# Where the operands of a float32r MLP start in SBUF, with a fourth buffer for v, stores planned on their own and an earlier guard

## The chip, the cores and the metric

The kernel runs on one core of a Trainium2 chip. The metric is the device time of one execution in microseconds. Before the change the median of three runs is 556.32 us (555.0 to 556.47). The profile shown here is of one more execution, which took 556.87 us, 554.8 us of it between its first and its last instruction (the span); the other 2.1 us lie around the span.

## The reference

The reference is a linear attention with decay (B=4 sequences, H=8 heads, S=768 tokens, D=48 per head), whose output goes through an MLP of model width 384 and hidden width 2048.

```python
for t in range(S):
    cur = einsum('bhd,bhe->bhde', u * k[t], v[t])
    y[t] = einsum('bhd,bhde->bhe', r[t], state + cur)
    state = w[t] * state + einsum('bhd,bhe->bhde', k[t], v[t])
x = y as [3072 tokens, 384]
h = x @ w_in
g = where(h > 0, h, exp(min(h, 0)) - 1)
out = g @ w_out
```

All inputs and the output are float32 (the weights arrive as 64-bit floats and are converted in the kernel).

## The kernel before

**Tiling.** Time is cut into 6 blocks of 128 steps (the code's `c`). A block has 4 units, one a sequence, so there are 24 units; a unit does the attention of 128 steps for all heads, and the four units of a block give the 512 token columns on which the MLP of that block works.

**Attention of a unit.** The loads w, k, r, v (and rk from unit 8 on) go out on SP's queue. VectorE runs two scans over the decays (lines 344 and 354) and scales r and k (358 and 361). TensorE makes the scores pa_s (413); VectorE masks them into am (416); TensorE makes the output pa_y from am, v and the carried state (443), the transposes pa_t (421), and the outer products pa_u (460) that VectorE adds to the state (468). pa_y is split into xh, rounded to float32r (ScalarE, 449), and the remainder xl (VectorE, 453).

**MLP of a block.** Each of the 16 slices f of the hidden width is a step with two groups of nine matmuls. `g1` (227 to 229) makes ph from xh and xl: for each of three 128-row chunks, w_h with xh, w_h with xl, w_l with xh. The ELU runs on ScalarE and VectorE (233, 236, 239), and the result m is split into gh (243) and gl (247). `g2` (256 to 258) adds nine matmuls of the same pattern to three accumulators acc. The moving operand is 512 columns wide (2048 bytes of a partition); in blocks 0 and 1 the first 6 slices are done as two halves of 256 columns. The weights of slice f are converted while block 0 runs (487 to 509). When a block is done, acc is copied to o and stored (269, 270); in the kernel before, each store is issued by the same task as its copy, so it stands in SP's queue right where the copy stands in the order of work.

**The order of work** is written by a list scheduler in the kernel (`Plan.order`). Each operation is a task with an engine, a duration (`COST`), predecessors, buffers that it takes (`hold`, with the counts in `SLOTS`) and a due time worked back from `BEGINS`, the planned begins of the six blocks. The scheduler simulates the engines with these numbers, and the instructions are issued in the order that results, on SP's queue too. At run time nothing is reordered: an engine or queue waits at its next instruction.

**Where tiles lie.** Pools are laid out in SBUF in the order of their creation. In the program built from the kernel before, the first tile of a pool lies at byte 16,512 of each partition. From the sizes of the tiles follow these begins, as remainders of 2048 bytes; a w_h or w_l operand is one of the 512-byte pieces of its tile:

| operand | before | after |
|---|---|---|
| w_h, w_l (pieces of 512 bytes) | 128, 640, 1152, 1664 | 0, 512, 1024, 1536 |
| xh, xl of blocks 0, 2, 4 | 896, 896 | 0, 0 |
| xh, xl of blocks 1, 3, 5 | 1056, 1152 | 0, 0 |
| gh, gl (two buffers each) | 1088 | 0 |

**The guard.** A product of the decays that is too small would make the scans wrong; `flag` collects a sum per unit, and `guard` (511 to 516) adds the sums up and writes `good`. After the fast part every engine loads `good` (line 655) and branches past a slow general version of the kernel.

Of the kernel before, what the change touches and what calls it, by code (L numbers as in the profile page):

```python
# [64 lines left out]
BEGINS = (20.6, 125.1, 205.2, 299.0, 400.1, 445.7, 557.5)
SOON = 0.0
LEAD = 70.0
ND = 8  # L70
SLOTS = dict(w=2, k=3, r=3, rk=2, v=3, eg=2, md=2, am=2, kt=1, pa=3, wg=2, ph=2, m=2, gh=2, gl=2, x=2, acc=1, raw0=1, x0=1, x1=1, x1a=1, x1b=1)


class Plan:
# [15 lines left out]
    def order(self):  # L90
# [29 lines left out]
        server = 0.0  # L120
# [5 lines left out]
        while len(order) < len(ts):  # L126
            moved = False
            for e in ready:
# [3 lines left out]
                for k in ready[e]:  # L132
# [6 lines left out]
                    u = (t["late"], rank[k])  # L139
# [22 lines left out]
                end = now + t["dur"]  # L162
# [49 lines left out]
def mlp(nc, w_h, w_l, ps_acc, ps_h, ml, po, dst, last=False):  # L212
# [9 lines left out]
    def g1(s, x):  # L222
        f, lo, hi = s["f"], s["lo"], s["hi"]
        xh, xl = (z[:, :, lo:hi] for z in x)
        s["ph"] = ph = ps_h.tile([P, N], F32, tag="ph", name="ph")[:, 0:hi - lo]
        for k in range(NK):
            nc.tensor.matmul(ph, w_h[:, f, 0, k], xh[:, k, :], start=(k == 0), stop=False)  # L227
            nc.tensor.matmul(ph, w_h[:, f, 0, k], xl[:, k, :], start=False, stop=False)  # L228
            nc.tensor.matmul(ph, w_l[:, f, 0, k], xh[:, k, :], start=False, stop=(k == NK - 1))  # L229
# [11 lines left out]
    def gh(s):  # L241
        s["gh"] = ml.tile([P, N], F32R, tag="gh", name="gh", bufs=2)[:, 0:s["hi"] - s["lo"]]
        nc.scalar.copy(s["gh"], s["m"])  # L243

    def gl(s):
        s["gl"] = ml.tile([P, N], F32R, tag="gl", name="gl", bufs=2)[:, 0:s["hi"] - s["lo"]]
        nc.vector.tensor_tensor(s["gl"], s["m"], s["gh"].bitcast(F32), ALU.subtract)  # L247

    def g2(s):
        f, lo, hi = s["f"], s["lo"], s["hi"]  # L250
        for m in range(NK):
            parts = 2 if (f == NF - 1 and m == NK - 1 and last) else 1
            for q in range(parts):
                s_ = slice(q * (hi - lo) // parts, (q + 1) * (hi - lo) // parts)
                a_ = accs()[m][:, lo + s_.start:lo + s_.stop]
                nc.tensor.matmul(a_, w_h[:, f, 1, m], s["gh"][:, s_], start=(f == 0 and lo == 0), stop=False)  # L256
                nc.tensor.matmul(a_, w_h[:, f, 1, m], s["gl"][:, s_], start=False, stop=False)  # L257
                nc.tensor.matmul(a_, w_l[:, f, 1, m], s["gh"][:, s_], start=False, stop=(f == NF - 1 and q == parts - 1))  # L258
# [3 lines left out]
    def out(m):  # L262
# [4 lines left out]
        for q in range(parts):  # L267
            s_ = slice(q * N // parts, (q + 1) * N // parts)
            (nc.vector.tensor_copy if last and (m == 1 or q) else nc.scalar.copy)(o[:, m, s_], acc[m][:, s_])
            nc.sync.dma_start(dst[m * P:(m + 1) * P, s_], o[:, m, s_])  # L270

    return dict(g1=g1, r1=r1, r2=r2, stt=stt, gh=gh, gl=gl, g2=g2, out=out)


@with_exitstack
def rwkv_elu_kernel(ctx, tc, wkr, rk, vp, u, uz, gkrw, gv, gu, w_in, w_out, out):
# [207 lines left out]
    def conv_a(f):  # L484
        g = stg.tile([P, 2, NK, P], U32, tag="wg", name="wg", bufs=2)
# [22 lines left out]
    def conv_l(f, eng):  # L508
        eng.tensor_tensor(w_l[:, f], raws[f][1].bitcast(F32), w_h[:, f].bitcast(F32), ALU.subtract)  # L509
# [19 lines left out]
    for u_ in units:  # L529
        i, c, b = u_["i"], u_["c"], u_["b"]  # L530
        early = max(0.0, BEGINS[c] - LEAD) if c > 0 else 0.0
        for n, kb in (("w", 232), ("k", 229), ("r", 229), ("rk", 393), ("v", 262)):
            if n == "rk" and i < ND:
# [9 lines left out]
        if i < ND:  # L543
# [4 lines left out]
            add(("md", i), "ACT", K["md"], lambda u_=u_: diag_out(u_), [("pd", i)])  # L548
            add(("sp", i), "ACT", K["spa"], lambda u_=u_: spread_act(u_), [("md", i), ("const",)])
        else:  # L550
            e1, e2 = ENG(i)
            for n, e, fn, dep in (("rk", e1, r_k, [("ld_rk", i)]), ("rku", e2, r_k_u, [("rk", i), ("ub",)])):
                add((n, i), e, K[n if e == "DVE" else "p" + n],
                    lambda u_=u_, fn=fn, e=e: fn(u_, nc.vector if e == "DVE" else nc.gpsimd), dep, lock=True)
            add(("dg", i), "DVE", K["dg"], lambda u_=u_: diag(u_), [("rku", i)])
            add(("sp", i), "POOL", K["sp"], lambda u_=u_: spread(u_), [("dg", i)], lock=True)
# [209 lines left out]
```

## Time and profile before

| | us |
|---|---|
| median of 3 runs | 556.32 (555.0 to 556.47) |
| profiled execution | 556.87 |
| its span | 554.8 |
| TensorE busy in the span | 519.8 |
| VectorE busy | 362.5 |
| ScalarE busy | 285.6 |
| GpSimd busy | 69.9 |
| mean granted TensorE clock | 0.974 of full |

PE is TensorE's matmuls, PEld its weight loads, DVE VectorE, ACT ScalarE, POOL GpSimd, SP the engine whose queue issues the transfers (SPq). A matmul's row in the timeline has its start, its duration and its line; the durations of neighbours overlap, so the rate of TensorE is read from the distance between starts. In a row of the windows view, each engine has its busy time and its count of instructions, then come the granted TensorE clock (PEclk), the DMA engines' busy share and GB/s.

### The profile page before, as it was taken

How to read it: one execution, taken by the hardware profiler on the slowest of the kernel's cores; microseconds unless marked ns; L12 is line 12 of the kernel's file. 1: busy time of each engine (PE TensorE's matmuls, PEld its weight loads, DVE VectorE, ACT ScalarE, POOL GpSimd, SP SyncE). 2: the span in 40 equal slices, each digit the busy share in tenths (PEclk: the TensorE clock that was granted, in tenths of full speed). 3: DMA queues.
4: the chain of work that ended last, by engine and by line, in shares of the span. 5: the costliest groups of instructions: out<-in, count | busy, mean ns of one | idle time of the engine just before them, and what ended most of it. 6: DMA issues, size and time to landing. Idle time of an engine off the chain costs nothing.

```text
span 554.8 us, 10007 instructions
## 1 busy us (share of the span) xinstructions
PE 519.8 (94%) x4065; PEld 430.3 (78%) x4065; DVE 362.5 (65%) x565; ACT 285.6 (51%) x558; POOL 69.9 (13%) x72
## 2 busy tenths in 40 slices
PE   5875999999999999999999999998799999999993
PEld 5765898889998887787878788876578878888882
DVE  6899999998796375369377335987596345333331
ACT  3668587687665443455443445643274432534441
POOL 1000000000240011215002300704530001000000
PEclk9977999999999999999999999999699999999998
DMA  8863574034410036211036200226520011100001
GB/s 267 250 199 120 156 234 168 1 87 144 122 60 2 0 90 192 59 55 36 0 91 201 69 0 18 74 91 209 153 70 1 0 37 38 58 0 1 0 1 61
DMA packets 26739, 47.36 MB, mean 85 GB/s; under 512 B 2752, under 2 KB 9280, under 8 KB 26688
## 3 DMA queue, kind: packets, MB, share of 16 engines
q1 hardware_dynamic: 26688, 46.66, 27.3%
q8 instruction: 34, 0.56, 0.4%
q14 instruction: 17, 0.14, 0.1%
HBM read 41.93 MB, written 4.72 MB: 84 GB/s over the span
## 4 chain that ended last, share of the span: by engine, by line
PE 83%; DVE 7%; DMA 3%; issue 3%; ACT 2%; SPq 1%; DVEq 0%; ACTq 0%
PE acc L256 12%; PE ph L227 12%; PE ph L229 11%; PE ph L228 11%; PE acc L257 11%; PE acc L258 11%; PE pa_y L443 6%; PE pa_s L413 4%; PE pa_u L460 2%; DMA v<-in_vp_dram 1%; PE pa_d L385 1%; PE pa_t L421 1%; DMA ubd<-in_uz_dram 1%; DVE gl L247 1%; DVE am L416 1%
## 5 line engine op out<-in xcount | busy, mean ns | idle before, releaser
L239 DVE SCALAR_TENSOR_TENSOR m<-m,ph 128x512 f32<-128x512 f32 (+1 forms) x108 | 67.1, 624 | 106.2 <-ACT m L236 105.9
L227 PE MATMUL ph<-xh,w_h 128*128 128x512 f32 (+1 forms) x324 | 123.2, 380 | 3.6 <-ACT w_h L506 1.6
L233 ACT ACTIVATE m<-ph 128x512 f32<-128x512 f32 (+1 forms) x108 | 59.3, 549 | 124.0 <-PE ph L229 120.8
L229 PE MATMUL ph<-xh,w_l 128*128 128x512 f32 (+1 forms) x324 | 121.0, 373 | 1.9 <-DVE w_l L509 1.9
L256 PE MATMUL acc<-gh,w_h 128*128 128x512 f32 (+1 forms) x325 | 122.0, 375 | 0.0
L228 PE MATMUL ph<-xl,w_h 128*128 128x512 f32 (+1 forms) x324 | 121.1, 374 | 0.2
L257 PE MATMUL acc<-gl,w_h 128*128 128x512 f32 (+1 forms) x325 | 120.2, 370 | 0.0
L258 PE MATMUL acc<-gh,w_l 128*128 128x512 f32 (+1 forms) x325 | 120.0, 369 | 0.0
L247 DVE TENSOR_TENSOR gl<-m,gh 128x512 fp32r<-128x512 f32 (+1 forms) x108 | 70.8, 658 | 35.1 <-ACT gh L243 34.8
L243 ACT CAST gh<-m 128x512 fp32r<-128x512 f32 (+1 forms) x108 | 61.4, 570 | 49.9 <-DVE m L239 43.4
L227 PEld LDWEIGHTS ph<-xh,w_h 128*128 128x128 f32 x324 | 62.2, 192 | 17.8 <-DVE m L239 3.0
L229 PEld LDWEIGHTS ph<-xh,w_l 128*128 128x128 f32 x324 | 62.1, 192 | 13.4 <-DVE w_l L509 2.4
L256 PEld LDWEIGHTS acc<-gh,w_h 128*128 128x128 f32 x325 | 61.4, 189 | 12.7 <-issue 1.0
L228 PEld LDWEIGHTS ph<-xl,w_h 128*128 128x128 f32 x324 | 62.3, 192 | 11.4 <-DVE xl L453 0.8
L258 PEld LDWEIGHTS acc<-gh,w_l 128*128 128x128 f32 x325 | 61.4, 189 | 11.3
L257 PEld LDWEIGHTS acc<-gl,w_h 128*128 128x128 f32 x325 | 61.4, 189 | 11.3 <-DVE gl L247 0.3
L236 ACT ACTIVATE m<-m 128x512 f32<-128x512 f32 (+1 forms) x108 | 63.1, 584 | 3.1
L403 POOL TENSOR_SCALAR_AFFINE_SELECT am<-md 128x512 f32<-128x512 f32 x32 | 29.2, 934 | 221.7 <-PE pa_y L443 156.2
L416 DVE COPY_PREDICATED am<-upper,pa_s 128x512 f32<-128x512 uint32 x48 | 32.8, 737 | 13.0 <-PE pa_s L413 11.9
L368 POOL TENSOR_TENSOR rk<-rk 128x384 f32<-128x384 f32 x16 | 18.3, 1147 | 171.9 <-DMA rk<-in_rk_dram 171.9
L413 PE MATMUL pa_s<-r,k 48*128 48x128 f32 x384 | 31.9, 304 | 7.7 <-issue 6.4
L413 PEld LDWEIGHTS pa_s<-r,k 48*128 48x128 f32 x384 | 26.9, 204 | 13.4 <-issue 9.9
(61 smaller groups left out, 504.4 us busy)
## 6 DMA issues: line engine op xcount, KB each, us to landing
v<-in_vp_dram SPq DMA_DIRECT2D x24, 256.0 KB, 3.1
rk<-in_rk_dram SPq DMA_DIRECT2D x16, 384.0 KB, 3.7
w<-in_wkr_dram SPq DMA_DIRECT2D x24, 226.2 KB, 4.8
k<-in_wkr_dram SPq DMA_DIRECT2D x24, 224.0 KB, 3.1
r<-in_wkr_dram SPq DMA_DIRECT2D x24, 224.0 KB, 5.1
out_dram<-o SPq DMA_DIRECT2D x17, 256.0 KB, 2.1
wrawx<-in_w_in_dram SPq DMA_DIRECT2D x10, 384.0 KB, 3.9
wrawx<-in_w_out_dram SPq DMA_DIRECT2D x10, 384.0 KB, 4.5
```

What stands on the lines that cost most here:

```text
L227: nc.tensor.matmul(ph, w_h[:, f, 0, k], xh[:, k, :], start=(k == 0), stop=False)
L228: nc.tensor.matmul(ph, w_h[:, f, 0, k], xl[:, k, :], start=False, stop=False)
L229: nc.tensor.matmul(ph, w_l[:, f, 0, k], xh[:, k, :], start=False, stop=(k == NK - 1))
L233: act(s["m"], s["ph"], AF.Relu, scale=-1.0)
L236: act(s["m"], s["m"], AF.Exp, scale=-1.0)
L239: stt_(s["m"], s["m"], -1.0, s["ph"], ALU.add, ALU.max)
L243: nc.scalar.copy(s["gh"], s["m"])
L247: nc.vector.tensor_tensor(s["gl"], s["m"], s["gh"].bitcast(F32), ALU.subtract)
L256: nc.tensor.matmul(a_, w_h[:, f, 1, m], s["gh"][:, s_], start=(f == 0 and lo == 0), stop=False)
L257: nc.tensor.matmul(a_, w_h[:, f, 1, m], s["gl"][:, s_], start=False, stop=False)
L258: nc.tensor.matmul(a_, w_l[:, f, 1, m], s["gh"][:, s_], start=False, stop=(f == NF - 1 and q == parts - 1))
L413: nc.tensor.matmul(pa[q][:, p], u_["k"][rs, p, :], u_["r"][rs, p, :], start=True, stop=True)
```

## The change

Four things change together.

- **Begins.** The kept pool `kp` is created before `big`, takes in the small constants `lim`, `ident`, `upper` and `ubd`, and is filled up by a tile of 160 floats, so that w_h begins at a multiple of 2048. xh and xl get a pool of their own (`xp`) right behind the weights, gh and gl another (`gp`) behind that. The table above has the begins that result.
- **v.** `SLOTS` has four buffers for v in place of three, and a unit's `v` task comes after that of the unit before it in its block.
- **Stores.** For blocks 0 to 4 a store is a task of its own on SP, with a due time 20 us behind the begin of the next block; the buffer o is given back by the stores in the plan. In the last block the store of the first half of the third accumulator goes out on ScalarE's queue.
- **Guard.** Its due time is worked from the begin of the last block (`BEGINS[-2] + 15`) in place of the end (`BEGINS[-1] + 20`).

`BEGINS` has other numbers, and the first transfer of the plan starts at 1.0 us. Other new names have values that change nothing here: `COLS` is 128 (one pass of its loop), `FILL` is empty, `HALF`, `STAY` and `SWITCH` are 0, and `DIAG` and `SPREAD` say what `ND = 8` said. A wait for `wh` is added to what frees a `wg` buffer in the plan.

```diff
-BEGINS = (20.6, 125.1, 205.2, 299.0, 400.1, 445.7, 557.5)
+DMA_FIRST, DMA_ISSUE, DMA_LAT, DMA_RATE = 1.0, 0.45, 1.9, 215.0
+BEGINS = (16.7, 126.9, 219.0, 315.0, 381.0, 446.3, 528.1)
+COLS = 128
+PAD = 160
-SLOTS = dict(w=2, k=3, r=3, rk=2, v=3, ...)
+SLOTS = dict(w=2, k=3, r=3, rk=2, v=4, ...)
...
-            nc.tensor.matmul(ph, w_h[:, f, 0, k], xh[:, k, :], start=(k == 0), stop=False)
-            nc.tensor.matmul(ph, w_h[:, f, 0, k], xl[:, k, :], start=False, stop=False)
-            nc.tensor.matmul(ph, w_l[:, f, 0, k], xh[:, k, :], start=False, stop=(k == NK - 1))
+            for n, (w, x_) in enumerate(((w_h, xh), (w_h, xl), (w_l, xh))):
+                for z in range(0, P, COLS):
+                    nc.tensor.matmul(ph[z:z + COLS], w[:, f, 0, k, z:z + COLS], x_[:, k, :],
+                                     start=(k == n == 0), stop=(k == NK - 1 and n == 2))
...
-        s["gh"] = ml.tile([P, N], F32R, tag="gh", name="gh", bufs=2)[:, 0:s["hi"] - s["lo"]]
+        s["gh"] = gp.tile([P, N], F32R, tag="gh", name="gh", bufs=2)[:, 0:s["hi"] - s["lo"]]
...
-            nc.sync.dma_start(dst[m * P:(m + 1) * P, s_], o[:, m, s_])
+            if last:
+                (nc.scalar if m == NK - 1 and q == 0 else nc.sync).dma_start(dst[m * P:(m + 1) * P, s_], o[:, m, s_])
+    def store(m):
+        if not last:
+            nc.sync.dma_start(dst[m * P:(m + 1) * P], box["o"][:, m])
...
+    kp = keep("kp", 1)
     big = keep("big", 1)
-    kp = keep("kp", 1)
+    xp = pool("xp", 1)
+    gp = pool("gp", 2)
...
+    big.tile([P, PAD], F32, name="pad")
     w_h = big.tile([P, NF, 2, NK, P], F32R, name="w_h")
...
-    ident = cst.tile([P, P], F32, name="ident")
+    ident = kp.tile([P, P], F32, name="ident")
...
-            xts[c] = [at.tile([P, NK, N], F32R, tag=n + str(c % 2), name=n, bufs=1) for n in ("xh", "xl")]
+            xts[c] = [xp.tile([P, NK, N], F32R, tag=n + str(c % 2), name=n, bufs=1) for n in ("xh", "xl")]
...
+        if b:
+            after.append(("v", i - 1))
...
+            add(("store", c, m), "SP", DMA_ISSUE, lambda m=m, fns=fns: fns["store"](m), [("out", c, m)], due=BEGINS[c + 1] + 20, size=256)
...
-        hold("raw0", ("out", c, 0), [("out", c, m) for m in range(NK)])
-    add(("guard",), "PE", 0.3, guard, [("fl", i) for i in range(NU)], due=BEGINS[-1] + 20)
+        hold("raw0", ("out", c, 0), [("store", c, m) for m in range(NK)])
+    add(("guard",), "PE", 0.3, guard, [("fl", i) for i in range(NU)], due=BEGINS[-2] + 15)
```

More of the change, by code (lines that the diff above doesn't have):

```diff
@@ L138, in order @@
                         continue
-                    u = (t["late"], rank[k])
+                    u = (t["late"] + (STAY if e == "PE" and (k[0] in MODES) != (mode in MODES) else 0.0), rank[k])
                     if best is None or u < best[0]:
@@ L161, in order @@
                         users.setdefault(x, []).append(h)
-                end = now + t["dur"]
+                end = now + t["dur"] * (2.0 if e == "PE" and now < HALF else 1.0)
+                if e == "PE":
+                    end += SWITCH * (MODES.get(mode, 0) != MODES.get(k[0], 0))
+                    mode = k[0]
                 busy[e] = end
@@ L209, with mlp @@
 ROUNDS = value_rounds()
-def mlp(nc, w_h, w_l, ps_acc, ps_h, ml, po, dst, last=False):
+def mlp(nc, w_h, w_l, ps_acc, ps_h, ml, gp, po, dst, last=False):
     act, stt_ = nc.scalar.activation, nc.vector.scalar_tensor_tensor
@@ L255, in g2 @@
                 a_ = accs()[m][:, lo + s_.start:lo + s_.stop]
-                nc.tensor.matmul(a_, w_h[:, f, 1, m], s["gh"][:, s_], start=(f == 0 and lo == 0), stop=False)
-                nc.tensor.matmul(a_, w_h[:, f, 1, m], s["gl"][:, s_], start=False, stop=False)
-                nc.tensor.matmul(a_, w_l[:, f, 1, m], s["gh"][:, s_], start=False, stop=(f == NF - 1 and q == parts - 1))
+                for n, (w, g) in enumerate(((w_h, s["gh"]), (w_h, s["gl"]), (w_l, s["gh"]))):
+                    for z in range(0, P, COLS):
+                        nc.tensor.matmul(a_[z:z + COLS], w[:, f, 1, m, z:z + COLS], g[:, s_],
+                                         start=(f == n == 0 and lo == 0), stop=(f == NF - 1 and q == parts - 1 and n == 2))
     box = {}
@@ L409, in score @@
         u_["pa"] = pa = [ps_a.tile([P, NP, C], F32, tag="pa", name="pa_s") for q in range(2)]
+        for _ in range(FILL.get(("s", u_["i"]), 0)):
+            nc.tensor.matmul(pa[0][:, 0], ident, ident, start=True, stop=True)
         for p in range(NP):
@@ L506, in conv_h, with conv_l @@
         nc.scalar.copy(w_h[:, f], raws[f][1].bitcast(F32))
-    def conv_l(f, eng):
-        eng.tensor_tensor(w_l[:, f], raws[f][1].bitcast(F32), w_h[:, f].bitcast(F32), ALU.subtract)
+    def conv_l(f):
+        tt(w_l[:, f], raws[f][1].bitcast(F32), w_h[:, f].bitcast(F32), ALU.subtract)
     def guard():
@@ L532, in rwkv_elu_kernel @@
         for n, kb in (("w", 232), ("k", 229), ("r", 229), ("rk", 393), ("v", 262)):
-            if n == "rk" and i < ND:
+            if n == "rk" and DIAG[i] == "PE":
                 continue
@@ L548, in rwkv_elu_kernel @@
             add(("md", i), "ACT", K["md"], lambda u_=u_: diag_out(u_), [("pd", i)])
+        else:
+            e = DIAG[i]
+            for n, fn, dep in (("rk", r_k, [("ld_rk", i)]), ("rku", r_k_u, [("rk", i), ("ub",)])):
+                add((n, i), e, K[n if e == "DVE" else "p" + n],
+                    lambda u_=u_, fn=fn, e=e: fn(u_, nc.vector if e == "DVE" else nc.gpsimd), dep, lock=True)
+            add(("md", i), "DVE", K["dg"], lambda u_=u_: diag(u_), [("rku", i)])
+        if SPREAD[i] == "ACT":
             add(("sp", i), "ACT", K["spa"], lambda u_=u_: spread_act(u_), [("md", i), ("const",)])
         else:
[L551 to L556, printed above, removed]
+            add(("sp", i), "POOL", K["sp"], lambda u_=u_: spread(u_), [("md", i)], lock=True)
         add(("s", i), "PE", K["s"], lambda u_=u_: score(u_), [("rh", i), ("kh", i), ("sp", i)])
@@ L576, in rwkv_elu_kernel @@
         add(("a", f), "ACT", K["a"], lambda f=f: conv_a(f), [("raw", f, 0), ("raw", f, 1)])
[L577 to L580 removed]
+        add(("cand", f), "DVE", K["cand"], lambda f=f: conv_and(f), [("a", f)], lock=True)
         add(("cb", f), "DVE", K["cv"], lambda f=f: conv_b(f), [("cand", f)], lock=True)
@@ L588, in rwkv_elu_kernel @@
     for c in range(NC):
-        fns = mlp(nc, w_h, w_l, ps_acc, ps_h, ml, stg, out[:, c * N:(c + 1) * N], last=c == NC - 1)
+        fns = mlp(nc, w_h, w_l, ps_acc, ps_h, ml, gp, stg, out[:, c * N:(c + 1) * N], last=c == NC - 1)
         t = BEGINS[c]
@@ L595, in rwkv_elu_kernel @@
             dep = [("wl", f)] + [("xl", i) for i in ns] + [("xh", i) for i in ns]
-            add(("g1", n), "PE", K["g"] * part, lambda s=s, c=c, fns=fns: fns["g1"](s, xts[c]), dep + [("g1", n - 1)], due=t + K["g"] * part)
+            add(("g1", n), "PE", K["g"] * part, lambda s=s, c=c, n=n, fns=fns: fns["g1"](s, xts[c], [ident] * FILL.get(("g1", n), 0)), dep + [("g1", n - 1)], due=t + K["g"] * part)
             add(("r1", n), "ACT", K["r1"] * (part + 0.4) / 1.4, lambda s=s, fns=fns: fns["r1"](s), [("g1", n)])
@@ L632, in rwkv_elu_kernel @@
         hold(p, ("raw", f, 0), [("raw", f, 1), ("cb", f), ("cc", f)])
-        hold("wg", ("a", f), [("wl", f)])
+        hold("wg", ("a", f), [("wl", f), ("wh", f)])
         if p != "raw0":
@@ L706, in general @@
                 nc.vector.tensor_tensor(xl, xf, xh.bitcast(F32), ALU.subtract)
-                z = mlp(nc, w_h, w_l, ps_acc, ps_h, ml, ml, out[:, bass.ds(c * n, n)])
+                z = mlp(nc, w_h, w_l, ps_acc, ps_h, ml, ml, ml, out[:, bass.ds(c * n, n)])
                 for f in range(NF):
@@ L714, in general @@
                     z["out"](m)
+                    z["store"](m)
 _OUT = (DM, B * S)
```

55 lines of the change are left out of this document (25 added, 30 removed).

## The prediction

> **What bounds the kernel now.** I read the page's first part, then the engines' busy time cut at the first matmul of each block, then what TensorE waited for, then the distances between single matmuls.
>
> ```profile
> span 554.8 us, 10007 instructions
> PE 519.8 (94%) x4065; PEld 430.3 (78%) x4065; DVE 362.5 (65%) x565; ACT 285.6 (51%) x558; POOL 69.9 (13%) x72
> ```
>
> ```profile
> core 0: us, PE busy (x) PEld busy (x) DVE busy (x) ACT busy (x) POOL busy (x), PEclk, DMA share, GB/s
> ...
> 25.80:62.10 36.30, 25.96 (x244) 23.36 (x241) 34.31 (x54) 24.21 (x54) 0.00 (x0) 0.81 0.38 122
> 62.10:125.50 63.40, 62.66 (x483) 53.54 (x480) 61.37 (x97) 46.98 (x93) 0.00 (x0) 1.00 0.45 141
> 125.50:220.00 94.50, 93.53 (x939) 81.06 (x937) 66.34 (x111) 52.16 (x119) 14.96 (x16) 1.00 0.27 84
> 220.00:303.80 83.80, 82.92 (x657) 66.60 (x657) 53.51 (x81) 39.75 (x72) 18.20 (x16) 1.00 0.25 75
> 303.80:395.80 92.00, 86.33 (x673) 68.52 (x673) 56.12 (x84) 40.32 (x73) 23.81 (x22) 0.96 0.28 81
> 395.80:475.80 80.00, 80.00 (x609) 64.61 (x608) 48.62 (x75) 36.54 (x65) 10.62 (x10) 0.98 0.14 43
> 475.80:545.20 69.40, 69.40 (x303) 55.85 (x301) 22.08 (x32) 31.54 (x53) 0.00 (x0) 1.00 0.03 12
> ```
>
> These rows are block 0 in two parts and blocks 1 to 5. From block 1 on TensorE is the bound: it is busy nearly all the time, and VectorE is at 70% of a block at most (66.34 of 94.50), 32% in the last. Block 0 has a second bound: VectorE, which converts the weights there, is busy 34.31 of 36.30 us and 61.37 of 63.40. So a faster matmul pays in blocks 1 to 5 and hardly in block 0.
>
> ```profile
> PE pa_s L413 <- issue: 6.4, 1, 6.4
> PE pa_y L443 <- DMA v<-in_vp_dram: 4.3, 1, 4.3
> ```
>
> Of TensorE's waits the view names these two as the longest. The first is in block 0, the second, for a load of v, in block 3.
>
> **The rate of a matmul.** In the timeline of TensorE the first column is the start. These rows are the firsts of groups of nine matmuls, two rows 0.94 us apart with eight distances between them, and two rows in a stretch of half clock.
>
> ```profile
> 67.74 0.28 PE L227 MATMUL ph<-xh,w_h 128*128 128x256 f32 x1
> ...
> 68.68 0.28 PE L229 MATMUL ph<-xh,w_l 128*128 128x256 f32 x1
> ...
> 71.94 0.28 PE L256 MATMUL acc<-gh,w_h 128*128 128x256 f32 x1
> ...
> 72.96 0.28 PE L256 MATMUL acc<-gh,w_h 128*128 128x256 f32 x1
> ...
> 241.52 0.39 PE L227 MATMUL ph<-xh,w_h 128*128 128x512 f32 x1
> ...
> 243.56 0.39 PE L256 MATMUL acc<-gh,w_h 128*128 128x512 f32 x1
> ...
> 245.66 0.39 PE L227 MATMUL ph<-xh,w_h 128*128 128x512 f32 x1
> ...
> 247.72 0.39 PE L256 MATMUL acc<-gh,w_h 128*128 128x512 f32 x1
> ...
> 396.35 0.63 PE L228 MATMUL ph<-xl,w_h 128*128 128x512 f32 x1
> ...
> 398.91 0.60 PE L228 MATMUL ph<-xl,w_h 128*128 128x512 f32 x1
> ...
> 500.93 0.39 PE L227 MATMUL ph<-xh,w_h 128*128 128x512 f32 x1
> ...
> 503.02 0.39 PE L256 MATMUL acc<-gh,w_h 128*128 128x512 f32 x1
> ```
>
> Three things are to be seen. First, at half clock a 512-wide matmul comes every (398.91 - 396.35)/6 = 0.427 us; the same columns at full clock would take half, 213 ns. Second, at full clock none does: g1 of block 2 (xh and xl at 896) takes 2.04/9 = 227 ns in one step and 2.06/9 = 229 in the next, g1 of block 5 (1056 and 1152) 2.09/9 = 232, g2 (gh and gl at 1088) 2.10/9 = 233. The excess of 14 to 20 ns is absent at half clock, so it is not a fixed cost of an instruction in clock cycles; something that does not slow down with the clock feeds the array too slowly. Third, the excess goes with the begin of what streams: same instruction, shape and clock, and 227 against 233. The 256-wide ones come every 0.94/8 = 118 ns (x at 896) and 1.02/9 = 113 (g at 1088).
>
> **The begins.** What does a matmul cost with all operands at multiples of 2048? No row has it. Bounds: 213 below, the half of the slow rows; above, no gain (233), and for a collision worse than now, see the third rival. Between them: at begin 896 the second 256 columns of a 512-wide matmul cost 227 - 118 = 109 ns, the first 256 with everything fixed 118. If a good begin takes away the 9 ns by which the first half is dearer, a 512-wide one costs 218 and a 256-wide one 109. I take 218; it lies toward the lower bound, but the nearest row, 227, is already 6 ns under g2's with a begin that is no multiple of 2048, so a begin counts for that much at least.
>
> [...]
>
> The counts stand in the groups by line and shape:
>
> ```profile
> L227 PE MATMUL ph<-xh,w_h 128*128 128x512 f32 x252 | 100.8, 400 | 1.1 <-DVE m L239 0.9
> ...
> L227 PE MATMUL ph<-xh,w_h 128*128 128x256 f32 x72 | 22.3, 310 | 2.5 <-ACT w_h L506 1.6 <-DVE wraw L495 0.4 <-DVE m L239 0.4
> ```
>
> With lines 228 and 229, g1 has 3 x 252 = 756 wide and 216 narrow matmuls, and g2 as many: 144 wide in each of the blocks 2 to 5, 90 wide and 108 narrow in each of the blocks 0 and 1.
>
> - g1 of blocks 2 and 4: 288 x (229 - 218) = 3.2 us.
> - g1 of blocks 1, 3, 5: 378 x (232 - 218) = 5.3 us.
> - g2 of blocks 1 to 5: 666 x (233 - 218) = 10.0 us.
> - Narrow ones of block 1: 108 x (118 - 109) + 108 x (113 - 109) = 1.4 us.
> - Block 0 could give 90 x 11 + 90 x 15 ns and another 1.4 us, 3.7 in all, but VectorE has only 63.40 - 61.37 = 2.0 us to spare in its longer part. I take half of that, 1.0.
>
> That is 20.9 us. Of it I take 10% off, 2.1 us, for places where TensorE now comes before an operand of the attention is ready (bounds: nothing, and half; second rival). The other tiles move in SBUF too; no row parts the durations of VectorE or ScalarE by begin, so I take zero, and it would matter in block 0 alone.
>
> **v and the stores.** The stall in block 3 begins in SP's queue:
>
> ```profile
> SPq L338 <- PE pa_u L460: 109.5, 17, 48.0
> SPq L270 <- ACT o L269: 100.7, 11, 61.7
> ```
>
> SP's own waits: loads that wait until pa_u has read a v buffer, and stores that wait for ScalarE's copy. Behind a waiting one stands every later transfer. What follows in the timeline:
>
> ```profile
> 370.09 0.33 SPq L338 DMA_DIRECT2D v<-in_vp_dram  x1
> ...
> 383.85 0.63 SPq L338 DMA_DIRECT2D v<-in_vp_dram  x1
> ```
>
> ```profile
> 391.39 1.94 PE L443 MATMUL pa_y<-am,v 128*32 128x128 f32 x32 [4.34 <-DMA v<-in_vp_dram]
> 393.25 1.01 PE L421 MATMUL pa_t<-ident,k 112*128 112x112 f32 x4
> 394.94 0.88 PE L460 MATMUL pa_u<-v,kt 128*48 128x48 f32 x16 [0.68 <-ACT kt L425]
> 395.75 0.80 PE L227 MATMUL ph<-xh,w_h 128*128 128x512 f32 x1
> ...
> 399.58 0.40 PE L227 MATMUL ph<-xh,w_h 128*128 128x512 f32 x1
> ```
>
> A fourth buffer lets the load of 383.85 go right behind the one of 370.09, 13 us earlier; the 4.34 us go. So does what they cause: behind the stall the clock is at half (the rows of 396.35 and 398.91). The nine matmuls from 395.75 to 399.58 take 3.83 us where nine at 232 take 2.09 (1.7 us). The same three attention pieces also took longer than at full clock, and here I have to bound: between nothing and half of 1.94 + 1.01 + 0.88, 1.9 us; I take 1.4, since short pieces keep some fixed time. Together 4.3 + 1.7 + 1.4 = 7.4 us. Next after the stall come k for pa_t and xl for g1; both follow pa_y by TensorE's own order, so nothing is late there behind it.
>
> The stores are as many as before, 19; they move in SP's order only. A store waits for its copy at line 269; behind it stand loads of the next block, which the plan now orders by their due times. That can remove waits of TensorE or make one. The bounds are one wait of the size of the longest seen, 6.4 us, to either side (the new `BEGINS` moves all due times, the same bounds hold for it); I take zero. The order between the v tasks of a block adds no instruction.
>
> **The tail.**
>
> ```profile
> 544.21 0.28 PE L256 MATMUL acc<-gh,w_h 128*128 128x256 f32 x1
> ...
> 544.32 5.25 SPq L270 DMA_DIRECT2D out_dram<-o  x4
> ...
> 545.24 0.17 DVE L515 TENSOR_REDUCE tot<-pf 1x1 f32<-1x24 f32 x1 [2.99 <-PE pf L513]
> 545.44 0.14 DVE L516 TENSOR_SCALAR good<-tot 1x1 int32<-1x1 f32 x1
> 545.55 1.02 DVE L269 COPY o<-acc 128x512 f32<-128x512 f32 x2
> ```
>
> VectorE reaches the copies of the second accumulator only behind the guard's two instructions, which wait for TensorE's last matmul. With the guard in the last block the copy can start when the second accumulator is done; TensorE begins on the third at 544.21, and its matmuls overlap by some 0.2 us, so the copy starts about 545.55 - 544.45 = 1.1 us earlier, behind the first store at 544.32. SP then issues three stores rather than four. I take 1.1 us, bounds 0 and 2. Where the guard goes, VectorE is idle for 47 of 69 us, so its 0.31 us and the wait for pf hide; were that cover gone, they would cost 0.5.
>
> **Sum.** Against the profiled execution: 556.87 - (20.9 - 2.1) - 7.4 - 1.1 = 529.6. Its span of 554.8 has 2.1 us around it, taken as unchanged; the median of the runs is 0.55 us under the profiled time, so the forecast is 529.0 us.
>
> **Rivals.**
>
> *The begin doesn't matter.* The excess could come from what streams beside it, with 896 and 1088 differing by chance. For it: the narrow groups, where 1088 is faster (113) than 896 (118), the other way round than the wide ones. Against it: the wide ones at 896 are faster in whole groups of nine, and the begins of their weights are those of g2 too. Then 7.4 and 1.1 remain: 556.3 - 8.5 = 547.8. [...] 17%.
>
> *The plan holds it back.* The matmuls get faster, but TensorE runs into waits for VectorE and the loads, whose order is laid out for nine matmuls in `K["g"]` = 2.12 us. For it: block 0's VectorE rows. Against: VectorE is busy 61% to 70% in blocks 1 to 4. Half of the 20.9 lost: 556.3 - 10.4 - 8.5 = 537.4. 15%.
>
> *Collision, slower.* With the change the weight that is being loaded and the operand that streams begin at the same multiples of 512. If two reads in step disturb each other, each matmul's distance grows; price: the step that the trace has between two begins, 233 - 227 = 6 ns, but upward, on 1512 wide and 432 narrow (as half) matmuls, 1728 x 6 = 10.4 us, in block 0 too, where TensorE is busy 62.66 of 63.40. 556.3 + 10.4 - 8.5 = 558.2. It decides from 8.5/1728 = 4.9 ns a matmul. For it: every begin differs now from its weight's, and the excess is there only where the reading is fast. Against: the 227 and the 233 go with weights of the same four begins, so the pairing isn't what parts them now. 8%.
>
> **How the numbers follow.** The forecast has 60%, the rivals 17, 15 and 8. A change of this kernel of less than 0.3% (1.7 us) can't be told from none. Faster takes the forecast, the second rival and nearly all of the first: 0.88; within 0.3%: 0.04, the first rival with a new wait of 6.4 us; slower: 0.08. The forecast's own range: 213 in place of 218 gives 5 x 1332 = 6.7 us more and no loss to waits 2.1 more, so 520 at the low end, and a wait of 6.4 us more 536. The range reaches on to the first rival: 519 to 549.
>
> **What would show it.** Groups of nine wide matmuls in 1.96 us in g1 and g2 alike (right); 2.06 to 2.10 as before (first rival); above 2.10 (third). Blocks 2 and 5 shorter by about 144 x 11 + 144 x 15 and 288 x 15 ns, some 4 us each. In TensorE's waits no v above 1 us and no half clock behind block 3; a new name there with over 5 us would be the plan's. The two copies at line 269 in VectorE with no guard ahead of them. Wrong I would be above all if the distances stay near 230.

## The result, and the profile after

The changed kernel takes 543.07 us (median of four runs, 541.91 to 544.36) against 556.2 us (555.0 to 556.47) of the kernel before on the same chip: a ratio of 0.9769, with a 95% interval of 0.9742 to 0.9795. It is faster by 13.1 us. The forecast was 529.0 us, a gain of 27.3: the direction is right, and the time lies within the stated 519 to 549, but only because that range reached on to the first rival; 13.1 us were gained of 27.3. The profiled execution took 544.36 us, so it is the slowest of the four.

The page's first lines for the changed kernel:

```profile
span 542.6 us, 9986 instructions
...
PE 515.3 (95%) x4065; PEld 430.5 (79%) x4065; DVE 361.8 (67%) x565; ACT 284.6 (52%) x558; POOL 65.1 (12%) x72
...
PEclk8677799999999999999999999999999999999998
```

TensorE's busy time has fallen by only 4.5 us (519.8 to 515.3), where the forecast took some 20 us out of its matmuls. The same row of the page for the kernel before:

```profile
PEclk9977999999999999999999999999699999999998
```

The dip in its slice 29 (from 388 us), behind the wait for v, is gone after the change; in slices 1, 2 and 5, within the first 68 us, the clock is lower than it was.

The stretches between the first matmuls of the blocks, the changed kernel (start, blocks 0 to 5, tail):

```profile
0.00:25.90 25.90, 18.16 (x173) 15.71 (x173) 19.45 (x32) 13.78 (x31) 2.32 (x8) 0.74 0.91 277
25.90:129.40 103.50, 93.56 (x713) 81.03 (x712) 95.97 (x150) 72.84 (x157) 0.00 (x0) 0.90 0.42 129
129.40:224.50 95.10, 93.61 (x947) 80.85 (x947) 65.45 (x110) 49.15 (x108) 15.92 (x16) 1.00 0.22 66
224.50:307.80 83.30, 82.16 (x658) 66.59 (x657) 54.26 (x80) 40.01 (x72) 15.14 (x16) 1.00 0.26 75
307.80:389.60 81.80, 81.76 (x658) 66.60 (x656) 53.27 (x80) 39.85 (x73) 21.97 (x21) 1.00 0.36 105
389.60:467.80 78.20, 78.20 (x626) 63.94 (x625) 49.98 (x79) 37.13 (x66) 9.72 (x12) 1.00 0.16 51
467.80:535.70 67.90, 67.89 (x303) 55.81 (x301) 23.00 (x35) 31.43 (x52) 0.00 (x0) 1.00 0.03 13
535.70:542.60 6.90, 0.00 (x0) 0.00 (x0) 0.44 (x2) 0.37 (x1) 0.00 (x0) 0.76 0.33 120
```

Against the rows of before the span's 12.2 us come from these places: block 3 is 10.2 us shorter (92.0 to 81.8), the tail 2.7 (9.6 to 6.9), block 4 1.8, block 5 1.5, block 2 0.5; block 0 is 3.8 us longer (99.7 to 103.5), block 1 0.6 and the start 0.1. Block 5 holds the same 303 matmul records in both kernels, so its 1.5 us is what the begins gave there; the forecast had 4.2 for it (144 x 14 ns and 144 x 15 ns). The other blocks hold other amounts of attention work than before (658 records in block 3, not 673), so a block alone doesn't show what an edit did.

The rate, in the timeline of the changed kernel: the first two rows are matmuls of 256 columns, 12 apart; the others are the firsts of neighbouring groups of nine, 512 wide.

```profile
138.46 0.28 PE L263 MATMUL acc<-gl,w_h 128*128 128x256 f32 x1
...
139.90 0.28 PE L263 MATMUL acc<-gl,w_h 128*128 128x256 f32 x1
...
500.80 0.39 PE L233 MATMUL ph<-xh,w_h 128*128 128x512 f32 x1
...
502.84 0.39 PE L263 MATMUL acc<-gh,w_h 128*128 128x512 f32 x1
...
504.88 0.39 PE L233 MATMUL ph<-xh,w_h 128*128 128x512 f32 x1
```

g1 and g2 are equal now, 2.04/9 = 226.7 ns for a wide matmul. That is the 227 ns which g1 of block 2 had before at begin 896, and not the 218 of the forecast; a group of nine lies between the 1.96 us that would have shown the forecast right and the 2.06 that would have shown the first rival. A narrow one takes 1.44/12 = 120.0 ns, which is no less than before (118 and 113).

TensorE's longest waits in the changed kernel:

```profile
PE pa_s L429 <- issue: 3.3, 1, 3.3
PE acc L263 <- ACT gh L248: 2.6, 2, 1.9
PE pa_d L399 <- DVE rkc L394: 2.6, 2, 1.7
PE ph L233 <- DVE w_l L521: 2.2, 2, 1.2
```

v is gone from the list, and no new wait of over 5 us has come. The tail in its timeline (the stores on SP's queue and on ScalarE's, and VectorE's two copies):

```profile
534.95 2.20 SPq L277 DMA_DIRECT2D out_dram<-o  x3
535.02 0.69 DVE L275 COPY o<-acc 128x512 f32<-128x512 f32 x1 [1.55 <-PE acc L263]
...
536.13 0.38 ACTq L277 DMA_DIRECT2D out_dram<-o  x1
536.14 0.42 DVE L275 COPY o<-acc 128x256 f32<-128x256 f32 x1 [0.42 <-ACT o L275]
```

No guard stands ahead of the copies, and SP's row of three stores is 2.20 us long where that of four was 5.25. Such a row runs from the first issue to the end of the last, waits for the copies in between included.

### The profile page after: what moved, and what is told of

The parts are those of the page before. It is cut to its first block, busy times and chain, and to the rows that moved or that the text cites. A ratio compares the mean times of both kernels' runs of the same rounds, so it can differ in the third digit from the quotient of the medians.

```text
span 542.6 us, 9986 instructions
## 1 busy us (share of the span) xinstructions
PE 515.3 (95%) x4065; PEld 430.5 (79%) x4065; DVE 361.8 (67%) x565; ACT 284.6 (52%) x558; POOL 65.1 (12%) x72
## 4 chain that ended last, share of the span: by engine, by line
PE 79%; DVE 9%; DMA 6%; ACT 3%; issue 2%; SPq 0%; DVEq 0%; ACTq 0%
PE acc L263 33%; PE ph L233 32%; PE pa_y L459 6%; PE pa_s L429 4%; ACT am L410 2%; DMA k<-in_wkr_dram 1%; PE pa_u L476 1%; DMA wrawx<-in_w_out_dram 1%; DMA r<-in_wkr_dram 1%; PE pa_t L437 1%; DVE am L432 1%; DMA w<-in_wkr_dram 1%; DVE eg L368 1%; DVE w_l L521 1%; DVE eg L358 1%
## 5 line engine op out<-in xcount | busy, mean ns | idle before, releaser
L244 DVE SCALAR_TENSOR_TENSOR m<-m,ph 128x512 f32<-128x512 f32 (+1 forms) x108 | 67.3, 624 | 99.5 <-ACT m L241 99.0
L233 PE MATMUL ph<-xh,w_h 128*128 128x512 f32 (+1 forms) x324 | 121.7, 376 | 0.8 <-DVE m L244 0.7
L233 PE MATMUL ph<-xh,w_l 128*128 128x512 f32 (+1 forms) x324 | 119.6, 369 | 2.2 <-DVE w_l L521 2.2
L233 PE MATMUL ph<-xl,w_h 128*128 128x512 f32 (+1 forms) x324 | 119.5, 369 | 0.0
L252 DVE TENSOR_TENSOR gl<-m,gh 128x512 fp32r<-128x512 f32 (+1 forms) x108 | 73.0, 678 | 35.0 <-ACT gh L248 34.3
L263 PEld LDWEIGHTS acc<-gh,w_h 128*128 128x128 f32 x325 | 62.7, 193 | 15.4 <-ACT gh L248 3.0
L263 PEld LDWEIGHTS acc<-gl,w_h 128*128 128x128 f32 x325 | 62.7, 193 | 11.8 <-DVE gl L252 2.4
L263 PEld LDWEIGHTS acc<-gh,w_l 128*128 128x128 f32 x325 | 62.8, 193 | 9.9
L417 POOL TENSOR_SCALAR_AFFINE_SELECT am<-md 128x512 f32<-128x512 f32 x32 | 21.0, 680 | 199.0 <-PE pa_y L459 128.8
L382 POOL TENSOR_TENSOR rk<-rk 128x384 f32<-128x384 f32 x16 | 20.1, 1258 | 189.6 <-DMA rk<-in_rk_dram 189.5
```

Source lines behind the costliest of these rows:

```text
L233: nc.tensor.matmul(ph[z:z + COLS], w[:, f, 0, k, z:z + COLS], x_[:, k, :], start=(k == n == 0), stop=(k == NK - 1 and n == 2))
L244: stt_(s["m"], s["m"], -1.0, s["ph"], ALU.add, ALU.max)
L263: nc.tensor.matmul(a_[z:z + COLS], w[:, f, 1, m, z:z + COLS], g[:, s_], start=(f == n == 0 and lo == 0), stop=(f == NF - 1 and q == parts ...
L382: eng.tensor_tensor(u_["rk"][:, 0], u_["rk"][:, 0], u_["rk"][:, 1], ALU.mult)
L417: nc.gpsimd.affine_select(out=am, in_=u_["md"][:, q::2].unsqueeze(2).broadcast_to([P, NP, C]), pattern=[[0, NP], [1, C]], compare_op=ALU.i ...
```

## The experiments

The experiments ran in three groups, each beside the kernel before on the same chip; its medians were 556.67, 556.9 and 557.38 us. A ratio is that of an experiment to the kernel before of its group, with a 95% interval behind it.

### The parts alone

**The begins alone.** The kernel before with the SBUF layout of the change and nothing else; the order of instructions on every engine stays as it was.

```diff
-    big = keep("big", 1)
     kp = keep("kp", 1)
+    big = keep("big", 1)
+    xp = pool("xp", 1)
+    gp = pool("gp", 2)
...
+    big.tile([P, 160], F32, name="pad")
```

> The kernel before with the new begins alone: pools, fill-up tile and pads as in the change, every engine's order of instructions as before. Floor theory: a wide matmul at a good begin costs 226.7 ns, the value that the best steps of before had already (16 columns of 512 + 32), so blocks 1 to 5 gain 288 x 2.4 + 378 x 5.7 + 666 x 6.7 ns = 7.3 us, block 0 next to nothing, the stall for v in block 3 stays: 548 to 550 us. Forecast as recorded (218 ns): 535 to 538 us. No-effect theory (the gain is the plan's): 555 to 557 us. In the trace: g1 and g2 at 226.7 ns in every undisturbed group of nine (floor theory).

Measured: 550.12 us (549.54 to 552.94), ratio 0.9893 (0.9865 to 0.9921): 6.5 us less, with bounds of 4.4 and 7.5. Its timeline in block 5:

```profile
495.44 0.39 PE L227 MATMUL ph<-xh,w_h 128*128 128x512 f32 x1
...
497.48 0.39 PE L256 MATMUL acc<-gh,w_h 128*128 128x512 f32 x1
...
499.51 0.39 PE L227 MATMUL ph<-xh,w_h 128*128 128x512 f32 x1
```

and its wait for v, which stays:

```profile
PE pa_y L446 <- DMA v<-in_vp_dram: 3.9, 1, 3.9
```

The same 2.04 us for nine. The begins do matter, so the first rival falls, and they matter by a third of what the forecast took.

**The change without the begins.** The changed kernel, with its order of instructions, but each operand at the begin that it had before.

```diff
-    kp = keep("kp", 1)
     big = keep("big", 1)
+    kp = keep("kp", 1)
     xp = pool("xp", 1)
+    xp1 = pool("xp1", 1)
+    xp2 = pool("xp2", 1)
+    kpc = pool("kpc", 1)
     gp = pool("gp", 2)
+    xp1.tile([P, 40], F32, name="pad1")
+    xp2.tile([P, 24], F32, name="pad2")
...
-    big.tile([P, PAD], F32, name="pad")
```

> The changed kernel with the old begins (weights at 128, x at 896 and at 1056 and 1152, g at 1088), every engine's order as in the changed kernel. Floor theory: the 7.3 us come back, 549 to 551 us, with groups of nine at 229 to 233 ns. No-effect theory: 542 to 544 us.

Measured: 548.87 us (548.67 to 549.07), ratio 0.9861 (0.9837 to 0.9884). The changed kernel's ratio is 0.0092 lower, 5.1 us. Single wide matmuls are back at 229 ns (x at 896), 232 (x at 1056 and 1152) and 233 (g at 1088), medians over the groups of nine of the whole trace.

**Four buffers for v alone.**

```diff
-SLOTS = dict(w=2, k=3, r=3, rk=2, v=3, ...)
+SLOTS = dict(w=2, k=3, r=3, rk=2, v=4, ...)
```

> The kernel before with a fourth buffer for v alone (only SP's order differs, TensorE's is the same). Stall theory: the 4.3 us wait in block 3 and the half clock behind it go, 7.4 us: 548 to 550 us. Rival, the stall moves to another load (r or k of the next block) behind the same stores: 553 to 557 us.

Measured: 550.65 us (549.66 to 553.12), ratio 0.9902 (0.9875 to 0.9929): 6.0 us less, with bounds of 4.0 and 7.0. TensorE at the place of the stall:

```profile
387.30 0.84 PE L443 MATMUL pa_y<-r,st 112*32 112x128 f32 x24
387.96 1.06 PE L443 MATMUL pa_y<-am,v 128*32 128x128 f32 x32
388.95 0.60 PE L421 MATMUL pa_t<-ident,k 112*128 112x112 f32 x4
390.23 0.59 PE L460 MATMUL pa_u<-v,kt 128*48 128x48 f32 x16 [0.68 <-ACT kt L425]
390.74 0.50 PE L227 MATMUL ph<-xh,w_h 128*128 128x512 f32 x1
...
392.92 0.39 PE L227 MATMUL ph<-xh,w_h 128*128 128x512 f32 x1
```

pa_y goes on without a wait; it and the pieces behind it take 1.06, 0.60 and 0.59 us where they took 1.94, 1.01 and 0.88, and nine matmuls of g1 take 2.18 us (390.74 to 392.92) where they took 3.83. The wait for kt, 0.68 us, is there as it was. In the kernel before, the row that stands ahead of the wait is

```profile
386.21 0.84 PE L443 MATMUL pa_y<-r,st 112*32 112x128 f32 x24
```

From that piece to the tenth matmul of g1 the kernel before takes 399.58 - 386.21 = 13.37 us, and this one 392.92 - 387.30 = 5.62: 7.75 us less at the place itself. That price is of one execution. In the profile of the tail alone, further down, the stall is there too, with a wait of 3.52 us, and the same stretch takes 397.84 - 386.09 = 11.75 us, 6.13 more than here, with two matmuls at half clock still to come.

**The tail alone.** The guard's due time and the one store on ScalarE's queue.

```diff
-            nc.sync.dma_start(dst[m * P:(m + 1) * P, s_], o[:, m, s_])
+            (nc.scalar if last and m == NK - 1 and q == 0 else nc.sync).dma_start(dst[m * P:(m + 1) * P, s_], o[:, m, s_])
...
-    add(("guard",), "PE", 0.3, guard, [("fl", i) for i in range(NU)], due=BEGINS[-1] + 20)
+    add(("guard",), "PE", 0.3, guard, [("fl", i) for i in range(NU)], due=BEGINS[-2] + 15)
```

> The kernel before with the tail's two edits alone: the guard's due time from the last block's begin, and the last block's store of the third accumulator's first half on ScalarE's queue. From the last MLP matmul to the end the changed kernel takes 7.2 us where the kernel before takes 10.0. Tail theory: 2.8 us, 553 to 554 us. Rival as recorded (1.1 us): 555 us. If the 2.8 came from elsewhere: 556 us.

Measured: 554.66 us (553.04 to 555.98), ratio 0.9962 (0.9946 to 0.9978): 2.0 us less. Its tail:

```profile
543.12 1.97 SPq L270 DMA_DIRECT2D out_dram<-o  x3
543.21 0.69 DVE L269 COPY o<-acc 128x512 f32<-128x512 f32 x1 [2.16 <-PE acc L258]
```

The copy starts 0.09 us behind the first store; it was 1.23 (544.32 to 545.55). That is the 1.1 us of the forecast. SP is done with issuing 1.97 us behind its first store, and was 5.25; the earlier copy has a part in that, since SP's second store waits for it. What is left of the 2.0 us is put down to the store that SP no longer issues; the guard and the store were not run apart.

**The three parts together**, without stores as tasks, the order of the v tasks and the new `BEGINS`; its edit is the three above together.

> The kernel before with its own plan and begins of blocks, and three parts of the change: the new begins, the fourth v buffer, the tail's two edits; without the stores as tasks, the order between v tasks and the new numbers of the plan. If the parts add up, 6.5 + 6.0 + 2.0 us under 556.7: 542 us, and the rest of the change (the re-planned order) is worth nothing against 543.1 for the whole. If the re-planned order gives some of the gain: 545 us or more; if it costs some, as its block 0 suggests (3.8 us longer than before): 538 to 541.

Measured: 542.76 us (541.61 to 545.09), ratio 0.9756 (0.9728 to 0.9784). The parts' gains add up: 6.5 + 6.0 + 2.0 = 14.5, against 556.9 - 542.76 = 14.1. And it is the whole change's ratio of 0.9769 within both intervals: the re-planned order, with all that goes with it, gave nothing that can be told from zero.

The spans by blocks (us, each from its first matmul of g1 to that of the next block):

| | start | 0 | 1 | 2 | 3 | 4 | 5 and tail |
|---|---|---|---|---|---|---|---|
| before | 25.8 | 99.7 | 94.5 | 83.8 | 92.0 | 80.0 | 79.0 |
| begins alone | 26.1 | 99.4 | 93.6 | 83.2 | 89.4 | 79.3 | 76.4 |
| v alone | 25.2 | 101.0 | 94.0 | 83.8 | 86.7 | 78.3 | 78.5 |
| tail alone | 25.5 | 99.5 | 94.0 | 83.9 | 90.9 | 80.5 | 77.0 |
| three parts | 26.6 | 99.4 | 93.6 | 83.1 | 85.0 | 77.3 | 74.9 |
| change, old begins | 25.5 | 103.3 | 95.6 | 83.5 | 83.1 | 79.1 | 76.7 |
| change | 25.9 | 103.5 | 95.1 | 83.3 | 81.8 | 78.2 | 74.8 |

The two kernels with the re-planned order have a block 0 of over 103 us and a shorter block 3; with the old order and the new begins block 0 stays at 99.4. So the longer block 0 doesn't come from the begins. Whether it comes from the order alone is open: the granted clock between 20 and 60 us is 0.71 in the profile of the change and 0.83 in that of the three parts, and v alone, with the old order and 0.76, has 101.0. The shorter block 3 holds less work (658 records for 672) and doesn't pay for it: blocks 1 to 4 together take 338.4 us in the change and 339.0 in the three parts.

### What makes a begin good

The begins alone showed a gain that ends at the 227 ns which one old begin (896) had reached already. So what is it that counts? Three theories: a multiple of 2048, as the change has it; a begin high enough or at a multiple of some smaller size; or the place of the streaming operand against the weight that is loaded meanwhile, since 896 - 128 = 3 x 256. An operand that begins a multiple of 256 bytes from the weights is called in step here, any other out of step. The five kernels below have the layout of the begins alone, with paddings that set the begins one by one (gh and gl take two buffers with different begins in turn); the order of instructions is that of the kernel before.

```diff
-    big.tile([P, 160], F32, name="pad")
+    big.tile([P, 192], F32, name="pad")
...
-    xp = pool("xp", 1)
-    gp = pool("gp", 2)
+    xp1 = pool("xp1", 1)
+    xp0 = pool("xp0", 1)
+    gp = (pool("gp0", 1), pool("gp1", 1))
+    xp1.tile([P, 480], F32, name="pad1")
```

This is the third of them; 192 puts the weights at 128, and 480 the rest at 0 (192 in its place: at 896).

| kernel | weights | x of odd, even blocks | gh and gl, in turn |
|---|---|---|---|
| low begins | 0 | 64, 128 | 256, 512 |
| high begins | 0 | 768, 1024 | 1280, 1536 |
| weights at 128 | 128 | 0, 0 | 0, 0 |
| weights at 128, the rest at 896 | 128 | 896, 896 | 896, 896 |
| weights at 64, the rest at 320 | 64 | 320, 320 | 320, 320 |

> The kernel with the new begins alone, weights at 0, but xh and xl at 64 in blocks 1, 3, 5 and at 128 in blocks 0, 2, 4, gh and gl at 256 and 512 in turn. If the begin of what streams counts: groups of nine above 226.7 ns (229 to 233) for those that are no multiple of 2048. If the begin of the weights counts: 226.7 in all. If a start a little above a boundary is the bad case (64 and 128, as 1088 and 1056 were): g1 at 232, g2 at 227.

Measured: 555.31 us (one run). g1 takes 229.0 ns with x at 64 and 232 to 233 with x at 128; g2, at 256 and 512, takes 229.8 behind x at 128 and 231.6 behind x at 64 (medians over the trace). In block 5, with x at 64:

```profile
496.37 0.40 PE L230 MATMUL ph<-xh,w_h 128*128 128x512 f32 x1
...
498.43 0.40 PE L261 MATMUL acc<-gh,w_h 128*128 128x512 f32 x1
...
500.51 0.40 PE L230 MATMUL ph<-xh,w_h 128*128 128x512 f32 x1
```

> As the one before, with xh and xl at 768 in blocks 1, 3, 5 and at 1024 in blocks 0, 2, 4, gh and gl at 1280 and 1536 in turn. If the begin of what streams counts by 2048: 229 to 233 ns in all. If by 1024: 226.7 in g1 of the even blocks alone. If by the weights: 226.7 in all. Any group below 226 would say that 226.7 is no floor and the forecast's 218 could be had.

Measured: 551.4 us (one run); 226.6 to 226.8 ns in all groups, though none of these begins is a multiple of 2048. Its timeline:

```profile
494.99 0.39 PE L261 MATMUL acc<-gh,w_h 128*128 128x512 f32 x1
...
497.03 0.39 PE L230 MATMUL ph<-xh,w_h 128*128 128x512 f32 x1
...
499.07 0.39 PE L261 MATMUL acc<-gh,w_h 128*128 128x512 f32 x1
```

> The kernel with the new begins, but the weights' tiles at 128 again, every fourth piece across a multiple of 2048; x and g at 0. If only what streams counts: 226.7 ns in all groups of nine, and a time as with all new begins (550 us). If the weights count: 229 to 233 ns and 555 us.

Measured: 556.61 us (one run). All that streams lies at multiples of 2048, and the gain is gone; nine take 2.10 and 2.09 us:

```profile
496.11 0.40 PE L261 MATMUL acc<-gh,w_h 128*128 128x512 f32 x1
...
498.21 0.39 PE L230 MATMUL ph<-xh,w_h 128*128 128x512 f32 x1
...
500.30 0.39 PE L261 MATMUL acc<-gh,w_h 128*128 128x512 f32 x1
```

> The kernel before in all but its begins: weights at 128 as before, but x and g all at 896, so 768 = 3 x 256 bytes from the weights' begin. Relative theory (what counts is that the streaming operand begins a multiple of 256 bytes away from the weight pieces, not where either begins): 226.7 ns in all undisturbed groups of nine and 549 to 551 us, as with all at multiples of 2048. Absolute theory (weights have to begin at a multiple of 512 and x and g at one of 256): 229 to 233 ns and 555 to 557 us, as with weights at 128 and x and g at 0.

Measured: 550.97 us (548.91 to 552.03), ratio 0.9876 (0.9844 to 0.9908), the gain of the begins alone, with nothing at a multiple of 2048:

```profile
495.51 0.39 PE L261 MATMUL acc<-gh,w_h 128*128 128x512 f32 x1
...
497.56 0.39 PE L230 MATMUL ph<-xh,w_h 128*128 128x512 f32 x1
...
499.60 0.39 PE L261 MATMUL acc<-gh,w_h 128*128 128x512 f32 x1
```

> As the one before, with weights at 64 and x and g at 320, 256 apart. Relative theory: 226.7 ns. If relative, but only for begins at multiples of 128: above 229 ns.

Measured: 550.09 us (one run), 226.6 to 226.8 ns in all groups:

```profile
496.64 0.39 PE L230 MATMUL ph<-xh,w_h 128*128 128x512 f32 x1
...
498.68 0.39 PE L261 MATMUL acc<-gh,w_h 128*128 128x512 f32 x1
...
500.72 0.39 PE L230 MATMUL ph<-xh,w_h 128*128 128x512 f32 x1
```

So of the three theories the third holds for the begins that were run: what counts is the distance from the begin of the weights (pieces of 512 bytes) to that of the streaming operand. At a multiple of 256 bytes (0 in the change, 256 and 768 in the last two kernels, 768 to 1536 in the high begins) a wide matmul takes 226.7 ns, at 64 beyond one 229, at 128 beyond one 232 to 233; in the kernel before, 160 beyond one (x at 1056) went with 232 and 192 (g at 1088) with 233. That it is the load of a weight, beside the stream, which makes the difference is argued and not shown: no run parts the load from the rest.

An operand in step doesn't reach 226.7 at once among others that are out of step. In the kernel before, g1 of blocks 2 and 4 (x at 896, in step) comes behind a g2 out of step: over 19 such groups its first five distances are 230.6 ns in the mean and its last four 227.0. In the low begins, g2 of the same blocks has 231.5 and 226.8; behind x at 64, in blocks 1, 3 and 5, it stays at 231.7 up to the ninth, and why it doesn't recover there is open. Within a group it is the same: xl of the odd blocks of the kernel before is in step (1152 - 128 = 4 x 256) and yet takes 231 ns and more between xh's at 1056.

### Where the missing gain could still be

**No halves in block 1.** The halves save waiting for a half-done group but cost narrow matmuls, which have got no faster (120.0 ns, where half of a wide one is 113.4). The three parts together, with the six slices of block 1 undivided:

```diff
-FH = (6, 6)
+FH = (6, 0)
```

> The kernel with three parts of the change (542.8 us), with block 1's six slices as 512-wide steps in place of halves (FH = (6, 0)), which makes 108 wide matmuls at 226.7 ns of 216 narrow ones at 120 ns: 1.4 us less on TensorE. If TensorE sets the pace there: 541 us. If the halves are needed since they can start when two units of the block are ready: 544 us or more.

Measured: 560.64 us (559.13 to 565.83), ratio 1.0082 (1.0048 to 1.0116): 18 us slower than the three parts with the halves. Of TensorE's waits:

```profile
PE pa_u L463 <- ACT kt L428: 4.6, 7, 0.7
PE pa_s L416 <- DVE k L364: 4.5, 3, 3.0
```

Most of the loss is early: the first matmul of block 1 comes at 148.1 us, and at 126.0 with the halves; that of block 2 at 238.2 against 219.6. That fits halves which can start on two units of a block, but no run shows which wait costs how much.

**A plan for the new rate.** The second rival said that the order of work, made for nine matmuls in 2.12 us, holds the faster ones back. The three parts together with the plan told the measured 2.04:

```diff
-COST = dict(..., g=2.12, ...)
+COST = dict(..., g=2.04, ...)
```

> The kernel with three parts of the change (542.8 us), with nine matmuls planned at their measured 2.04 us in place of 2.12. Rival of the prediction (the plan made for slower matmuls holds them back): 538 to 540 us. If the plan's rate doesn't matter: 541 to 545 us.

Measured: 552.12 us (551.46 to 553.07), ratio 0.9912 (0.9889 to 0.9935): 9 us slower than with the old number, so neither expectation came. Block 1 in the windows of this kernel:

```profile
125.00:226.90 101.90, 99.67 (x995) 86.01 (x993) 65.18 (x114) 53.40 (x121) 20.56 (x20) 0.97 0.32 96
```

and of the three parts with 2.12:

```profile
126.00:219.60 93.60, 92.89 (x939) 81.62 (x937) 65.29 (x111) 52.00 (x119) 16.02 (x16) 1.00 0.28 84
```

One of TensorE's waits, of this kernel and then of the three parts:

```profile
PE pa_u L463 <- ACT kt L428: 4.8, 7, 1.1
```

```profile
PE pa_u L463 <- ACT kt L428: 2.0, 3, 0.7
```

The order that comes out puts more into block 1 (995 records against 939), has some half clock there (0.97), and waits for kt 4.8 us in seven places in place of 2.0 in three. Which of its moves costs the 9 us isn't settled. What it shows is that the true rate in the plan is no remedy; an order written for 2.04 by other means wasn't tried.

## Why the prediction was right or wrong

**The rate of a matmul: here it failed.** The step is "If a good begin takes away the 9 ns by which the first half is dearer, a 512-wide one costs 218 and a 256-wide one 109". A good begin doesn't take the 9 ns away. With all operands in step a wide matmul costs 226.7 and a narrow one 120.0, so the second 256 columns cost 106.7, which is half of the 213.3 that the half-clock rows give. What is left, 13.3 ns, is the same for a wide and a narrow one: a fixed time of these matmuls at full clock, at both widths. The prediction had ruled out a fixed cost in clock cycles, because the half-clock rows don't have it, and took all of the excess for slow feeding; that was the wrong conclusion from a right reading. What the 13.3 ns are, and why they are absent at half clock, no run here settles. It had also read the 118 as an excess of the first half. That row came from 896, in step but in turn with a g2 out of step at 113; where all is in step narrow matmuls take 120.0, so they were a little faster before.

With the measured floor in the prediction's own counts: 288 x (229 - 226.7) + 378 x (232 - 226.7) + 666 x (233 - 226.7) = 0.7 + 2.0 + 4.2 = 6.9 us, less 108 x (120 - 118) + 108 x (120 - 113) = 1.0 for the narrow ones of block 1, makes 5.9. The begins alone gave 6.5. The term was put at 18.8 (20.9 less 10%), so 12.3 us of the 14.2 by which the forecast missed the gain are this one number. The counts and the blocks were right, and the lower end of it stood on the page: 227 at 896 was the nearest row, and it was the floor. The 229 of the next step, which went into the sum, was the same rate behind a disturbed start (230.6 in the first five distances, 227.0 in the last four). No begin that was run brings a wide matmul under 226.6.

**The begin as such.** The prediction and the change speak of multiples of 2048; the runs show the distance to the weights, modulo 256 bytes. The third rival had the two reads as a pair, but with the sign turned: in step is good, out of step costs 2 to 7 ns. Its sentence against itself, "the pairing isn't what parts them now", is refuted: 227 at 896 and 233 at 1088 differ because 896 is 3 x 256 from weights at 128 and 1088 is not at any such place. The first rival, that the begin doesn't matter, is refuted by the begins alone and by the change without them. It was right in one thing: the part of the excess that can be taken away (2 to 7 ns) hangs on where the weights begin too. With the weights at 128, x and g at 0 give 232 to 233 ns and at 896 226.7, and with the weights at 0, x and g at 0 give 226.7; the mechanism behind that the runs don't show.

**v.** Right in mechanism and in size. At the place itself 7.75 us are gone, by the rows above: 391.39 - 386.21 less 387.96 - 387.30, 4.5 us, for the wait; 4.36 less 2.78, 1.6, for the three pieces; 3.83 less 2.18, 1.65, for nine matmuls of g1. The forecast had 4.3 + 1.4 + 1.7 = 7.4. Over the runs the fourth buffer alone gives 6.0 us, with bounds of 4.0 and 7.0; its block 0 is 1.3 us longer in the profile, with a granted clock of 0.76 between 20 and 60 us against 0.83 before. Nor does the stall cost the same each time: 7.75 us in the profile of before and 6.13 in that of the tail alone.

Half clock stood behind the wait of 4.34 us (0.51 granted from 389.0 to 399.4 us). At the same place with four buffers, where only the 0.68 us for kt are left, the matmuls of g1 come every 0.23 us from the second on.

**The tail.** Right, and too small: 1.1 us for the guard is what the rows show, but "SP then issues three stores rather than four" stood there without a price. The other 0.9 of the 2.0 is put down to it, without a run of its own.

**Stores, `BEGINS`, the order of v: put at zero.** Together they gave nothing that can be told from zero: the three parts without them have the change's time. One by one they were not run. The second rival's waits didn't come: TensorE is busy 81.76 of 81.80 us in block 3, 78.20 of 78.20 in block 4 and 67.89 of 67.90 in block 5. The gain isn't lost behind the matmuls; it wasn't there.

**The sum.** Forecast 18.8 + 7.4 + 1.1 = 27.3; measured alone 6.5 + 6.0 + 2.0 = 14.5; the three together 14.1, the whole change 13.1.

Open is why block 0 of the re-planned order is longer in its profiles (the mean granted clock of the changed kernel's four runs goes from 0.965 to 0.984, and the profiled one has the lowest, so the half clock isn't the same in executions of one order either), and which move of the plan costs what in the last two experiments.

## What to carry to other kernels

When a stream of float32r matmuls sits some nanoseconds above what its columns cost (here 227 to 233 ns against 213.3), read the distance of single matmuls for each pair of begins, and lay every streaming operand a multiple of 256 bytes from the weights, which gave 226.7 at each such pair run here; among them, the absolute begins didn't matter. Before forecasting a rate below the best undisturbed row of a trace, take that row as the floor unless two widths, both undisturbed, say otherwise. A wait of some 4 us on TensorE (4.34 and 3.52) cost 6 to 8 us (7.75 and 6.13), since half clock followed, and was worth a buffer. The order written by the plan is brittle: a truer number in it made the kernel 9 us slower.

## What the runs showed of the hardware

- Streaming and weights out of step (modulo 256 bytes) cost a 512-wide float32r matmul 2 ns at 64 bytes (229.0) and 6 at 128 (232 to 233); in step, with all that streams, it took 226.7 ns at each of the pairs run (0 and 0; 0 and 768 to 1536; 64 and 320; 128 and 896).
- A group in step behind one out of step started 4 to 5 ns a matmul slower and was back at 227 after five matmuls, behind x at 128 (231.5, then 226.8; weights at 0) and behind g at 1088 (230.6, then 227.0; weights at 128); behind x at 64, with weights at 0, it stayed 5 ns slower for all nine (231.7).
- At full clock, in step, a float32r matmul took 13.3 ns beside its columns' time (213.3 for 512, half of the 427 at half clock), at 512 and at 256 columns (226.7 and 120.0); at half clock (0.50 granted from 396.3 to 399.0 us) the 427 ns for 512 columns left nothing for it.
- A wait of TensorE of 4.34 us, up to 391.39, brought half clock (0.51 granted from 389.0 to 399.4 us) and cost 7.75 us at its place; one of 3.52 us cost 6.13 by the same measure.
- At the end SP's row of four stores was 5.25 us long, its rows of three 1.97 and 2.20, waits for the copies included.
